# Dummy matmuls between the opening dummies and the first cumulative sum of a gated-linear-attention and expert kernel

## The chip, the cores and the metric

The kernel runs on one core of one Trainium2 chip. The metric is the device time of one execution in microseconds (us). The engines are TensorE (PE; its weight loads are listed as PEld), VectorE (DVE), ScalarE (ACT), GpSimd (POOL) and SyncE (SP), which issues the DMAs of this kernel in order.

## What is computed

Two stages follow each other: a recurrent attention with a decay for every channel, over 4 batches x 8 heads x 768 steps x 48 channels, and a feed-forward block with a squared ReLU over its 3072 x 384 output.

```python
def _attn_ref(q, k, v, alpha):
    state = np.zeros((B, H, D, D))
    for t in range(S):
        state = alpha[:, :, t, :, None] * state + np.einsum('bhd,bhe->bhde', k[:, :, t], v[:, :, t])
        y[:, :, t] = np.einsum('bhd,bhde->bhe', q[:, :, t], state)
    return y

def _moe_ref(x, w_in, w_out):      # x 3072x384, w_in 384x2048, w_out 2048x384
    r = np.maximum(x @ w_in, 0.0)
    return (r * r) @ w_out
```

## The kernel before

**Chunks.** The 4 x 768 steps are cut into 24 chunks of 128 steps. In a chunk the decay becomes a cumulative sum: ACT takes the logarithm of alpha, PE multiplies it with a triangle of ones (`e_p0`), ACT takes the exponentials A and 1/A of the sum, and DVE scales q with A (`qA_s`, L431) and k with 1/A (`kI_s`, L434). PE transposes both (L241), ACT or DVE copies the transposes out (`qkT`, L369 and L371), PE forms the scores (`sc`), DVE masks them (`sm`, L472), and PE multiplies them with v, adding the part of the running state (`st`). The result is copied (`xn`), transposed and copied again (`xT_big`).

**The first four chunks** belong together: their alpha is one load in two halves, laid out so that each chunk occupies 32 of the 128 partitions, four steps to a partition. ACT takes the logarithm of each half (L324, into a part of a `gT` tile), and each chunk's cumulative sum is four accumulating matmuls of 32 rows and 384 columns against the stationary `tri` (tile name of `tri4`). The sums of chunks 0 and 1 are the first real work of PE; they wait for both logarithms. Two PSUM banks (`GLA_BANKS`, banks 0 and 1) serve all attention work, so the sums of chunks 2 and 3 wait until a bank has been read.

**Feed-forward.** Groups of token tiles go through `x @ w_in` (banks 2 to 4), ReLU on ACT (L576), square on DVE (L584), and `@ w_out` (banks 4 to 2). The weights come as float32 through four staging buffers shared with the first alpha load, and are cast by DVE or ACT (L292, L294) into `w_in_b` and `w_out_b`; a weight piece's load is issued only when the buffer that it reuses has been cast. The first four chunks' q, k and v are loaded ahead of the weights.

**Order.** A planner (`Plan.run`) simulates all engines with durations written into the operations, and sorts the operations by planned start; `plan.order` is then issued engine by engine in exactly that sequence. Operations carry a planned `start` and `dur` in us. A DMA load of the first alpha has a planned duration of 1.18 us, a latency of 2.0 us and an earliest start of 0.6; a joint logarithm has 0.7 us, ACT's latency is 0.14 and the slack in front of PE 0.05.

**Dummies.** In front of all planned work PE gets seven matmuls of 128 x 512 zeros (`warm`) into bank 4, whose result nobody reads. In the emission loop at the end of the kernel, between two consecutive PE operations, further dummies of 256 columns are issued: as many as fit, at 0.11 us each, into the planned gap less 0.2 us. This ends with the first `@ w_out` operation. `pe_end`, the planned end of the previous PE operation, starts as None, so that nothing is issued in front of the first one. PE instructions are recorded at the helper's line, L238 for matmuls and L241 for transposes.

## Time and profile before

| what | value |
|---|---|
| median of 3 runs | 194.79 us (193.36 to 195.24) |
| the profiled execution, its own time | 194.11 us |
| its span, first to last instruction | 192.4 us |
| mean granted TensorE clock | 0.973 |
| PE's share of the chain that ended last | 79% |
| HBM read, written | 25.17 MB, 4.72 MB |

The span is the time between the first and the last instruction of the profiled execution; the 1.71 us to its own time lie outside. A busy share is the time in which an engine had at least one instruction under way; matmuls are pipelined, and the ends shown are modelled. The granted clock is TensorE's as a share of full speed, where the profiler recorded a change of it. In a timeline line the columns are start and duration in us, engine, line, operation, output and input tiles, their shape and how many; a bracket gives the idle time in front and what ended it.

### The profile page before, as it was taken

To read this page: it belongs to the slowest core of one execution; us is meant where nothing else is said; L and a number is where in the kernel's file an instruction comes from. 1 tells how busy PE (TensorE), PEld (TensorE's weight loads), DVE (VectorE), ACT (ScalarE), POOL (GpSimd) and SP (SyncE) were. 2 spreads that over 40 slices of the span, in tenths; PEclk is the share of its full clock that TensorE was granted. 3 is DMA by queue.
4 is the path that set the end of the run, shared out by engine and by line. 5 is a ranking of instruction groups with operands and counts; after the bars stand their busy time and mean duration, and the time that the engine had idled before them with its cause. 6 is when DMAs were issued, how large, how long until landed. Compare 5 with 4: busy or idle time off the path is not lost.

```text
span 192.4 us, 4966 instructions
## 1 busy us (share of the span) xinstructions
PE 182.6 (95%) x1946; PEld 132.3 (69%) x1947; DVE 127.9 (66%) x280; ACT 125.1 (65%) x289; POOL 17.7 (9%) x43
## 2 busy tenths in 40 slices
PE   6599899999998999999999999999999999999992
PEld 2256664566886788867868868867868768768651
DVE  1356988883799897967758758758757767734200
ACT  4654698917896778966956956956955845718310
POOL 8122000001102111112110110110110000000000
PEclk9855999999999999999999999999999999999999
DMA  6999689898999899999999998460110110111012
GB/s 182 222 217 283 245 250 309 202 306 173 243 202 203 175 237 187 217 215 222 212 215 237 189 218 178 95 174 3 43 44 2 42 45 0 44 41 44 22 59 82
DMA packets 104327, 30.20 MB, mean 157 GB/s; under 512 B 96240, under 2 KB 103152, under 8 KB 104304
## 3 DMA queue, kind: packets, MB, share of 16 engines
q1 hardware_dynamic: 104304, 29.89, 66.4%
q8 instruction: 15, 0.25, 0.5%
q14 instruction: 8, 0.07, 0.1%
HBM read 25.17 MB, written 4.72 MB: 155 GB/s over the span
## 4 chain that ended last, share of the span: by engine, by line
PE 79%; DMA 12%; ACT 3%; DVE 2%; issue 1%; SPq 0%; POOL 0%; POOLq 0%; ACTq 0%
PE bank L238 65%; PE bank L241 7%; DMA wo<-in_moe_w_out_dram 7%; PE sc L238 4%; DMA vt<-in_v_dram 3%; DMA at<-in_alpha_dram 2%; PE st L238 2%; DVE gT L584 1%; DVE w_out_b L292 1%; DVE sm L472 1%; ACT qkT L369 1%; ACT xn L369 1%; ACT gT L324 0%; ACT w_in_b L294 0%; POOL vb L388 0%
## 5 line engine op out<-in xcount | busy, mean ns | idle before, releaser
L238 PE MATMUL bank<-xT_big,w_in_b 128*128 128x256 bf16 (+3 forms) x587 | 75.3, 270 | 0.3
L238 PE MATMUL bank<-w_out_b,gT 128*128 128x384 bf16 x384 | 71.4, 326 | 0.0
L576 ACT ACTIVATE r<-bank 128x512 bf16<-128x512 f32 (+2 forms) x100 | 57.0, 585 | 17.6 <-PE bank L238 14.8
L238 PEld LDWEIGHTS <-w_in_b 128*128 128x128 bf16 x588 | 49.7, 97 | 10.3 <-issue 0.7
L238 PEld LDWEIGHTS <-gT 128*128 128x128 bf16 x400 | 35.7, 98 | 19.2
L584 DVE TENSOR_TENSOR gT<-r 128x512 bf16<-128x512 bf16 (+2 forms) x100 | 39.2, 419 | 14.6 <-ACT r L576 14.5
L472 DVE TENSOR_TENSOR sm<-sc,utri_b 128x512 bf16<-128x512 f32 x48 | 30.8, 683 | 4.8 <-PE sc L238 4.8
L616 ACT COPY ob<-bank 128x384 f32<-128x384 f32 x23 | 11.0, 478 | 24.0 <-PE bank L238 24.0
L431 DVE TENSOR_TENSOR qA_s<-qt,A 128x384 bf16<-128x384 f32 x24 | 13.7, 570 | 18.8 <-ACT A L408 18.8
L388 POOL CAST vb<-vt 128x384 bf16<-128x384 f32 x24 | 13.0, 543 | 124.3 <-DMA vt<-in_v_dram 77.0
L371 DVE COPY qkT<-bank 128x1024 bf16<-128x1024 bf16 (+1 forms) x23 | 15.0, 655 | 6.7 <-PE bank L241 6.5
L238 PEld LDWEIGHTS <-qkT 64*128 64x128 bf16 (+1 forms) x272 | 11.1, 97 | 7.2 <-issue 2.7
L408 ACT ACTIVATE A<-bank 128x384 bf16<-128x384 f32 x24 | 11.9, 498 | 5.0 <-PE bank L238 5.0
L434 DVE TENSOR_TENSOR kI_s<-kt,Ainv 128x384 bf16<-128x384 f32 x24 | 13.5, 563 | 0.0
L497 ACT CAST sb<-st 128x384 bf16<-128x384 f32 x20 | 9.5, 477 | 6.0 <-DVE st L492 5.7
L369 ACT CAST xn<-bank 128x384 bf16<-128x384 f32 x24 | 11.5, 481 | 2.7 <-PE bank L238 2.6
L412 ACT ACTIVATE Ainv<-bank 128x384 bf16<-128x384 f32 x24 | 12.0, 501 | 0.0
L379 ACT ACTIVATE L_s<-at 128x384 bf16<-128x384 f32 x20 | 10.4, 522 | 1.6 <-DMA at<-in_alpha_dram 1.3
L492 DVE TENSOR_TENSOR st<-st,ae_s 128x384 f32<-128x384 f32 x20 | 11.2, 558 | 0.2 <-PE st L238 0.2
L371 DVE COPY xT_big<-bank 128x384 bf16<-128x384 bf16 x22 | 7.7, 352 | 4.5 <-PE bank L241 4.5
L241 PE MATMUL bank<-ident_bf,kI_s 128*128 128x128 bf16 x96 | 9.9, 230 | 0.4 <-ACT qkT L369 0.4
L241 PE MATMUL bank<-ident_bf,qA_s 128*128 128x128 bf16 x96 | 10.0, 230 | 0.0
(52 smaller groups left out, 139.5 us busy)
## 6 DMA issues: line engine op xcount, KB each, us to landing
qt<-in_q_dram SPq DMA_DIRECT2D x24, 192.0 KB, 3.9
kt<-in_k_dram SPq DMA_DIRECT2D x24, 192.0 KB, 3.8
vt<-in_v_dram SPq DMA_DIRECT2D x24, 192.0 KB, 3.9
out_dram<-ob SPq DMA_DIRECT2D x24, 192.0 KB, 2.8
at<-in_alpha_dram SPq DMA_DIRECT2D x20, 192.0 KB, 4.1
wo<-in_moe_w_out_dram SPq DMA_DIRECT2D x4, 768.0 KB, 7.6
wi<-in_moe_w_in_dram SPq DMA_DIRECT2D x3, 768.0 KB, 8.1
at<-in_alpha_dram SPq DMA_DIRECT2D x2, 384.0 KB, 3.6
```

Source lines behind the costliest of these rows:

```text
L238: pin(nc.tensor.matmul(*a, **kw))
L241: pin(nc.tensor.transpose(*a))
L369: pin(nc.scalar.copy(out_t, in_t))
L371: pin(nc.vector.tensor_copy(out_t, in_t))
L388: pin(nc.gpsimd.tensor_copy(d["vb"], d["vt"]))
L408: pin(nc.scalar.activation(d["A"], d["pm"][:, 0:HD].rearrange("p (h d) -> p h d", h=H), AF.Exp))
L412: pin(nc.scalar.activation(d["Ai"], d["pm"][:, 0:HD].rearrange("p (h d) -> p h d", h=H), AF.Exp, scale=-1.0))
L431: pin(nc.vector.tensor_mul(qA[:, :, 0:D], d["qt"], d["A"]))
L434: pin(nc.vector.tensor_mul(kI[:, :, 0:D], d["kt"], d["Ai"]))
L472: pin(nc.vector.tensor_mul(d["sm"][:, hh], d["sc"][:, hh], utri_b.to_broadcast([P, NP, P])))
L576: pin(nc.scalar.activation(box["r"][:, 0:w], box["ph"][:, 0:w], AF.Relu))
L584: pin(nc.vector.tensor_mul(gT[g][:, f0:f0 + per, lo * P:lo * P + n], r, r))
```

## The change

`pe_end` no longer starts as None but as a planned time of 4.2 us, the constant `WARM_END`. The condition in the emission loop therefore holds for the first PE operation as well, and the loop issues dummies of 256 columns, from a fresh tile of bank 4, between the seven opening dummies and that operation. The plan is finished when this code runs, and isn't changed.

```diff
     plan.run(gate)
 
 
+    WARM_END = 4.2
     wp = banks[4].tile([P, 512], FP32, name="bank4")
     for _ in range(7):
         mm(wp, lhsT=warm[:, 0:P], rhs=warm, start=True, stop=True)
-    pe_end = None
+    pe_end = WARM_END
     for op in plan.order:
         if op.eng == "PE":
             if getattr(op, "moe", (0,))[0] == 2:
```

The loop's lines that follow, unchanged:

```python
                pe_end = None
                DUMMY = 0
            if pe_end is not None and DUMMY:
                n = max(0, int((op.start - pe_end - 0.2) / 0.11))
                if n:
                    wp = banks[4].tile([P, 512], FP32, name="bank4")
                for _ in range(n):
                    mm(wp[:, 0:256], lhsT=warm[:, 0:P], rhs=warm[:, 0:256], start=True, stop=True)
            pe_end = op.start + op.dur
        op.emit()
```

## The prediction, on record before the result

> **What bounds the kernel now.** I read the page first. TensorE (PE) is busy 95% of the span and carries 79% of the chain of waits; the slices show it saturated nearly everywhere, and its clock at half in one early stretch only.

> ```profile
> span 192.4 us, 4966 instructions
> ...
> PE 182.6 (95%) x1946; PEld 132.3 (69%) x1947; DVE 127.9 (66%) x280; ACT 125.1 (65%) x289; POOL 17.7 (9%) x43
> ...
> PEclk9855999999999999999999999999999999999999
> ```

> Each digit is 4.81 us: slices two to four hold the half clock. Next, busy time by window, finely, to find where the clock changes (columns: busy us of PE, weight loads, DVE, ACT, POOL; granted clock; DMA share; GB/s):

> ```profile
> 8.32:8.36 0.04, 0.04 (x2) 0.04 (x1) 0.04 (x1) 0.04 (x1) 0.00 (x0) 1.00 1.21 226
> 8.36:8.40 0.04, 0.04 (x2) 0.04 (x1) 0.04 (x1) 0.04 (x1) 0.00 (x0) 0.71 1.33 245
> ...
> 18.60:18.64 0.04, 0.04 (x5) 0.04 (x6) 0.00 (x0) 0.00 (x0) 0.00 (x0) 0.79 0.79 307
> ```

> The clock falls at 8.38 and is back at 18.62, 10.24 us later. I cut that stretch into thirds of 3.41 us, and lay the same cut on both sides:

> ```profile
> 1.55:4.96 3.41, 2.87 (x7) 0.85 (x6) 0.36 (x6) 1.37 (x2) 3.15 (x11) 1.00 0.92 266
> 4.96:8.38 3.42, 1.23 (x11) 0.71 (x11) 0.80 (x2) 2.16 (x5) 0.55 (x2) 1.00 1.22 225
> 8.38:11.79 3.41, 3.20 (x19) 1.77 (x18) 1.92 (x5) 1.77 (x4) 0.50 (x1) 0.50 1.21 215
> 11.79:15.20 3.41, 3.41 (x49) 2.24 (x48) 2.21 (x4) 2.29 (x6) 0.59 (x2) 0.50 1.14 214
> 15.20:18.62 3.42, 3.07 (x25) 2.24 (x25) 2.24 (x5) 1.55 (x3) 0.93 (x2) 0.50 0.99 288
> 18.62:22.03 3.41, 2.88 (x49) 2.15 (x50) 2.72 (x6) 1.83 (x4) 0.00 (x0) 1.00 1.02 384
> ```

> Last, the timeline of PE, for the paces behind those clocks:

> ```profile
> 1.26 3.17 PE L238 MATMUL bank<-warm 128*128 128x512 bf16 x7 [1.26 <-DVE warm L186]
> 6.22 0.83 PE L238 MATMUL bank<-gT,tri 32*128 32x384 bf16 x8 [1.79 <-ACT gT L324]
> 7.98 1.08 PE L238 MATMUL bank<-gT,tri 32*128 32x384 bf16 x4 [0.93 <-ACT Ainv L412]
> ...
> 10.88 1.46 PE L238 MATMUL bank<-gT,tri 32*128 32x384 bf16 x4 [0.21 <-DVE qkT L371]
> ...
> 17.13 1.49 PE L238 MATMUL bank<-warm 128*128 128x256 bf16 x6
> ...
> 19.12 1.04 PE L238 MATMUL bank<-warm 128*128 128x256 bf16 x8
> ```

> The clock column says 1.00 from the start, yet the paces correct it. Asked in finer steps, the opening dummies start at 2.51, 2.93, 3.36 and 3.79: 0.427 us for 512 columns, 1.2 columns per ns. The three sums that start at 7.98, 8.14 and 8.30 take 0.16 us for 384 columns, 2.4 per ns. So TensorE began at half pace, rose somewhere between 4.22 (end of the last opening dummy's columns) and 6.22, and fell at 8.38, after a window in which it worked 1.23 of 3.42 us (36%) although no pause in it exceeded 1.79 us. It kept full clock through the window from 18.62, with 2.88 of 3.41 (84%).

> [...]

> **The change part by part.** *How many dummies.* The plan starts its first PE operation when both halves of the joint logarithm are done: loads end at 0.6 + 2 x 1.18 + 2.0 = 4.96, the second logarithm at 5.66, with 0.14 latency and 0.05 slack 5.85. So n = int((5.85 - 4.2 - 0.2)/0.11) = int(13.2) = 13. Only this first operation is touched: every later one finds `pe_end` set as before. Plan, other engines' instructions and DMA issues stay in their order. The 13 write the bank 4 that the opening dummies wrote, on the same in-order engine; the repeated dummies of before, from 17.13 on, show no wait for that.

> *What they cost.* Cold, six take 1.49 us with about 0.21 of final drain: (1.49 - 0.21)/6 = 0.213 each. Warm, eight take 1.04 with 0.17: 0.109 each. The first starts at 4.22. All cold, the last one's columns end at 4.22 + 13 x 0.213 = 6.99; all warm, at 5.64. With the rise at 4.96, the cut's boundary before 8.38, 3.5 run cold and 9.5 warm: 4.96 + 9.5 x 0.109 = 6.00, or 6.17 with drain. The first sum started at 6.22, released by ACT, so in the profiled timing the cost is nothing: the wait of 1.79 us covers all 13. If that cover fails it is 6.99 - 6.22 = 0.77 us on the path. Other executions may rise at other times; between 0 and 0.77 I take 0.3.

> *What they buy.* The window 4.96 to 8.38 gains 1.04 us of matmul: 2.27 of 3.42, or 66%. Known: fall after 36%, hold after 84%; 66% is nearer to the hold (18 points against 30). The trace has no window between, so both ends stay in the range: no effect, or full clock from 8.38 to 18.62.

> *The worth of that stage.* Three windows hold 3.20 + 3.41 + 3.07 = 9.68 us of cold PE work, so it cannot exceed 4.84. On the chain: the third joint sum ran two of its four matmuls cold, 1.08 instead of 0.66, saves 0.42; eight transposes, 0.98 to 0.56 (four cost 0.34 with drain at 18.96 and 0.22 without), 0.42; the fourth sum, 1.46 to 0.74, 0.72; eight score matmuls, 0.54 to 0.34, 0.20. That makes 1.76 when DVE's masking of chunk 0 starts (12.99 now). From there DVE runs without pause to 17.49 on six steps, so PE's speed adds nothing along that engine. Then DVE idles 1.51 us, until the scores of chunk 2 at 18.55 (masking at 19.00). On PE's side, by the same paces, this stretch shortens by 0.55 + 0.20 + 0.15 + 0.20 + 0.25 + 0.60 = 1.95 (26 small matmuls, scores, state, two transposes, the six dummies), more than the idle time; so 1.51 is what can be had. Together 1.76 + 1.51 = 3.27 us at 19.0.

> Will the clock hold inside that stage? The work at double pace is about 4.84 us in 10.24 - 3.27 = 6.97, 69% busy, again between 36 and 84 and nearer to 84. [...]

> *How much reaches the end.* Next late are the loads. A staging buffer frees when DVE casts the first w_in piece (22.28 to 22.83), and the next piece is issued at 22.86; meanwhile the DMA engines drain. By one-microsecond windows they moved 385 GB/s at 21 to 22, 72 at 22 to 23, 29 at 23 to 24 and 152 at 24 to 25. The casts move 3.3 earlier with PE, but transfers only fill that hole of about 2.2 us. So loads come 2.2 earlier, PE wants them 3.27 earlier, and 1.1 must come out of slack. w_out: first cast done 33.05, first used 36.24; third done 41.68, used 43.52: slack 1.8, enough. Chunk loads: vt's cast ends at 38.78, its user starts 39.55: slack 0.77, loses 0.3; at 58.5 PE already waits 0.6 for a vt, with no slack. So 2.2 to 3.27 arrive; I take 2.6, about the mean less one small wait. After 60 us PE is full (40.00 of 40 us in 60:100 and in 100:140, and so on to 186), so nothing later can absorb or return it.

> Sum, against the profiled execution: 194.11 (span 192.4 and 1.71 around it) - 2.6 + 0.3 = 191.8. That execution lies 0.68 under the median of 194.79, inside the runs' 193.36 to 195.24; I don't scale, since a spread of that size would follow if before's early rise comes in only some executions, and that spread goes with the change.

> **The rivals.** *It falls anyway.* 66% is not enough, or the thinner windows behind it are not. For it: before fell with no long pause, and the 8.38 to 11.79 window is mostly transposes and 32-row sums, which at half clock were busy 3.20 of 3.41 us and did not bring the clock back, so busy time alone isn't what is counted. Against: the next cold window rose at 18.62 with only six dummies among small work. Fallen at 8.38: 194.1. Fallen at 11.79: saved 0.42 + 0.42 and about half of 0.72, some 1.2, less 0.3: 193.2. So 193.2 to 194.8 with the median's offset.

> *Late rise, slower than before.* The dummies delay the first joint sum. The last column ends at b + 0.51 x (6.99 - b) for a rise at b; this passes 6.22 when b is later than 5.42. Price 0.77 at most, at the head of the chain, where ACT, then PE wait for it; with the clock falling again nothing pays it back: 194.11 + 0.77 = 194.9, or 195.6 from the median. Against: in the profile the rise is before 6.22 even without the added work.

> *The loads take it.* The clock holds, but SP's queue, in order and with issues that last up to 4.13 us (qt at 26.36), keeps the loads where they were: the 3.27 shrink to what slack there is, 0.77 to 1.8: 192.6 to 193.6. Against: the buffers free earlier, and the 2.2 us hole is real.

> **How the numbers follow.** Hold: 0.55, 190.8 (3.27 arrives, no delay) to 192.7 (2.2, delay 0.77), likeliest 191.8. Falls anyway: 0.26. Late rise and slower: 0.12. Loads take it: 0.07. The range 190.6 to 194.8 takes in the first, second and fourth, and leaves out nearly the 0.12 and the tails. This kernel's measurement can tell about 1% from no change: 192.8 and 196.7 are the borders. Faster: the hold, less its edge, plus the better half of the loads case, 0.56. Slower by over 1% needs 1.95, more than the delay alone can give; 0.05 for the late rise together with a longer cold stretch. The rest, 0.39, lies within.

> **What would show it.** Thirteen more 128x256 matmuls between 4.2 and about 6.2, the first of them 0.213 apart, later ones 0.109; the first joint sum within 0.1 of 6.22; granted clock 1.00 through 8.38 and on to 19; the fourth joint sum about 0.7 long, not 1.46; masking of chunk 2 near 15.7, not 19.0; the DMA hole at 22 to 24 gone; PE's last matmul 2 to 3 us earlier. It is wrong if the clock falls at 8.4 or 11.8 anyway, if the first sum starts after 6.6, or if new PE waits on loads show between 30 and 60.

## The result, and the profile after

| | median, us | lowest to highest | executions |
|---|---|---|---|
| before | 194.78 | 193.13 to 196.09 | 20 |
| changed | 192.48 | 190.37 to 194.79 | 20 |

Over all 20 executions of each, the medians stand at 192.48/194.78 = 0.988: faster by about 1.2%. The ratio on record, 0.985 (95% interval 0.982 to 0.989), leaves out the six executions of the changed kernel above 193.2 us as slow ones, but by what follows these belong to it. The recorded 191.8 lay 0.7 us under the median, and the range held it.

The changed kernel's times do not scatter around one value. They fall into groups by the mean granted clock of the execution. With two repeats that are told below there are 32 executions:

| mean granted clock | executions | times, us | median |
|---|---|---|---|
| 0.999 to 1.000 | 13 | 190.37 to 192.10 | 190.89 |
| 0.989, 0.991 | 2 | 190.88, 192.37 | |
| 0.978 to 0.982 | 9 | 192.58 to 193.69 | 193.16 |
| 0.970 to 0.974 | 8 | 194.11 to 195.27 | 194.64 |

One third of before's cold stretch, 3.41 us at half clock, takes 3.41 x 0.5/192 = 0.009 off the mean, so the rows stand for none, one, two and three cold thirds.

The execution that was profiled took 193.69 us (span 192.0, clock 0.979): it is of the third group. Its page, the slices of the clock:

```profile
PEclk9957999999999999999999999999999999999998
```

Busy time by window, cut in thirds as in the prediction, but at this execution's own changes of clock (columns as there: PE, weight loads, DVE, ACT, POOL, granted clock, DMA share, GB/s):

```profile
2.84:6.25 3.41, 3.35 (x13) 1.69 (x12) 0.00 (x0) 1.68 (x2) 2.55 (x7) 1.00 1.06 279
6.25:9.66 3.41, 2.46 (x24) 1.35 (x22) 1.44 (x3) 1.84 (x5) 0.00 (x0) 1.00 1.03 203
9.66:13.07 3.41, 3.35 (x25) 1.66 (x23) 1.27 (x4) 1.81 (x5) 1.01 (x2) 0.50 1.04 203
13.07:16.49 3.42, 3.42 (x49) 2.80 (x49) 3.31 (x6) 1.98 (x6) 0.51 (x1) 0.50 1.03 208
16.49:19.90 3.41, 2.85 (x35) 2.03 (x34) 2.65 (x6) 2.29 (x5) 0.62 (x1) 1.00 0.98 293
```

Its timeline of PE, the lines that answer to those of before (the 20 `warm` are the seven opening dummies and the 13 added ones):

```profile
1.25 5.65 PE L238 MATMUL bank<-warm 128*128 128x512 bf16 x20 [1.25 <-DVE warm L186]
6.84 0.83 PE L238 MATMUL bank<-gT,tri 32*128 32x384 bf16 x8
8.62 0.81 PE L238 MATMUL bank<-gT,tri 32*128 32x384 bf16 x4 [0.94 <-ACT Ainv L412]
...
11.02 1.46 PE L238 MATMUL bank<-gT,tri 32*128 32x384 bf16 x4
```

Here the clock fell again, at 9.66, and was back at 16.49, after two thirds instead of three. The window in front of the fall had TensorE busy 2.46 of 3.41 us, 72%: more than the 66% that the prediction had hoped would do. And the first joint sum starts at 6.84, 0.62 late, without a releaser in its bracket: it stands behind the dummies. The end of PE's work came only 0.41 us earlier than in before's profile.

A second profile of the same kernel, from the repeat `e10_after` (190.52 us, span 188.8), caught an execution of the first group:

```profile
1.98:5.39 3.41, 3.35 (x11) 1.40 (x10) 0.10 (x2) 1.10 (x3) 3.16 (x10) 1.00 1.04 295
5.39:8.80 3.41, 2.46 (x22) 1.44 (x20) 1.00 (x3) 2.21 (x5) 0.12 (x1) 1.00 1.14 212
8.80:12.22 3.42, 2.87 (x33) 1.66 (x32) 2.25 (x6) 2.51 (x7) 0.50 (x1) 1.00 1.01 201
12.22:15.63 3.41, 2.90 (x54) 2.35 (x53) 3.41 (x8) 2.23 (x6) 0.81 (x2) 1.00 1.12 222
```

The clock stayed at full speed, behind a window with TensorE busy for the very same 2.46 us. So busy time alone does not tell these two apart. Its timeline, with the first sum only 0.20 late and the fourth at the full pace:

```profile
1.25 5.23 PE L238 MATMUL bank<-warm 128*128 128x512 bf16 x20 [1.25 <-DVE warm L186]
6.42 0.83 PE L238 MATMUL bank<-gT,tri 32*128 32x384 bf16 x8
8.20 0.81 PE L238 MATMUL bank<-gT,tri 32*128 32x384 bf16 x4 [0.95 <-ACT Ainv L412]
...
10.42 0.82 PE L238 MATMUL bank<-gT,tri 32*128 32x384 bf16 x4
...
15.87 0.40 PE L238 MATMUL sc<-qkT 64*128 64x128 bf16 x8
```

**What orders the windows.** Between two changes of the clock in the first 20 us lie 3.41 to 3.42, 6.82 to 6.83 or 10.24 us in the six profiles in which it fell early (before, after, `e1_again`, `e2_rows32`, `e4_half`, `e7_26`): one, two or three of the thirds that the prediction cut. So a third is taken here as the window of the count. That is the author's assumption: the traces show the lengths of the stretches, not what the clock is decided on. Weight each matmul's columns by the rows that it uses. In the window 5.39 to 8.80 of `e10_after`, about 8.7 dummies at the full pace (256/2.4 = 0.107 us each, at the 384 columns in 0.16 us of the joint sums) are 0.93 us of the whole array; the 12 joint sums take 0.16 us each on 32 of 128 rows, 0.48 us by weight; together 1.41 of 3.41, 0.41 by this rough count. In the window 6.25 to 9.66 of after, only 4.7 dummies were left (0.50), the same sums (0.48), and five transposes (0.27): 1.25, or 0.37. In before, 4.96 to 8.38: sums alone, 0.42, or 0.12. Done from each matmul's own start, which moves a share by about 0.01, over the profiles of this study:

```
weighted share of a window at full clock in these profiles, and what came after it
fell:  0.12 before   0.20 e2_rows32   0.28 e4_half   0.28 e7_26   0.38 after   0.39 e1_again
held:  0.40 e9_fill32   0.41 e3_fill   0.42 e10_after   and all others, 0.43 to 0.99
share of a window at half clock: stayed low up to 0.65, rose 0.75 to 1.01
```

Unweighted, the same matmuls fill 0.80 of after's window that fell and 0.60 of one in `e10_after` (12.22 to 15.63) that held; so the order is wrong without the rows, and right with them. Without the transposes it is wrong too: 0.18 held (`e10_after`, 8.80 to 12.22, 0.43 with them) and 0.35 fell (`e1_again`). So this count takes transposes like other matmuls.

This is an order found in the twelve profiles of this case, by the author's own count, not a mechanism or a threshold that was measured step by step. Its edge lies in the narrow gap between 0.385, which fell, and 0.403, which held, and a record of a matmul can be missing (`e10_after`'s page has 1959 of them, after's 1960). Rows were tested apart, in `e2_rows32` and `e9_fill32`.

The rise, where the record of the clock begins, came at 4.96 in before's profile, and at 6.25, 5.96 and 5.39 in the three profiles of the changed kernel, although the seven opening dummies start at 1.25 or 1.26 in all of them. In after's the paces agree: the dummies start 0.213 us apart up to 6.14 and 0.109 apart from 6.31 on. So the windows lay differently in these four executions. The rise at 6.25 left 4.7 dummies to the next window, and the clock fell; the rise at 5.39 left 8.7, and it held.

The dummies do a second thing. Of before's 57 executions beside the experiments, only 17 have a mean of 0.965 to 0.982, like the one that the prediction was worked out on. The other 40 have 0.996 and more and still took 193.34 us or longer; none of them was profiled, but an execution of this kind was (`e5_fill_only`, below), and its clock did not rise before 19.26. All 32 executions of the changed kernel are either in the groups of a fallen clock or, at 192.10 us and less, faster than any of before's. So behind the 13 dummies the early rise seems to come every time.

### The profile page after: what moved, and what is told of

Same layout as the page of the kernel before. It is cut to its first block, busy times and chain, and to the rows that moved or that the text cites. A ratio compares the mean times of both kernels' runs of the same rounds, so it can differ in the third digit from the quotient of the medians.

```text
span 192.0 us, 4993 instructions
## 1 busy us (share of the span) xinstructions
PE 184.0 (96%) x1960; PEld 133.4 (69%) x1960; DVE 127.2 (66%) x280; ACT 125.2 (65%) x289; POOL 17.6 (9%) x43
## 4 chain that ended last, share of the span: by engine, by line
PE 87%; ACT 4%; DMA 4%; DVE 3%; issue 1%
PE bank L238 73%; PE bank L241 8%; PE sc L238 4%; DMA wo<-in_moe_w_out_dram 4%; PE st L238 2%; ACT r L576 1%; DVE gT L584 1%; ACT xn L369 1%; DVE w_out_b L292 1%; DVE sm L472 1%; ACT qkT L369 1%; ACT sb L497 0%; ACT w_in_b L294 0%; DVE st L492 0%; ACT A L408 0%
## 5 line engine op out<-in xcount | busy, mean ns | idle before, releaser
L238 PE MATMUL bank<-xT_big,w_in_b 128*128 128x256 bf16 (+3 forms) x588 | 75.4, 270 | 0.2
L238 PE MATMUL bank<-w_out_b,gT 128*128 128x384 bf16 x384 | 71.4, 326 | 0.0
L238 PEld LDWEIGHTS <-w_in_b 128*128 128x128 bf16 x588 | 49.7, 97 | 10.3 <-issue 0.7
L238 PEld LDWEIGHTS <-gT 128*128 128x128 bf16 x400 | 35.7, 98 | 19.2
L584 DVE TENSOR_TENSOR gT<-r 128x512 bf16<-128x512 bf16 (+2 forms) x100 | 38.6, 412 | 14.9 <-ACT r L576 14.8
L371 DVE COPY qkT<-bank 128x1024 bf16<-128x1024 bf16 (+1 forms) x23 | 15.0, 655 | 6.8 <-PE bank L241 6.6
L238 PEld LDWEIGHTS <-qkT 64*128 64x128 bf16 (+1 forms) x272 | 11.1, 97 | 7.1 <-issue 2.4
L412 ACT ACTIVATE Ainv<-bank 128x384 bf16<-128x384 f32 x24 | 12.0, 499 | 0.0
L238 PE MATMUL bank<-warm 128*128 128x256 bf16 (+1 forms) x48 | 10.3, 357 | 1.3 <-DVE warm L186 1.3
L371 DVE COPY xT_big<-bank 128x384 bf16<-128x384 bf16 x22 | 7.7, 352 | 4.2 <-PE bank L241 4.0
L238 PE MATMUL bank<-vb,sm 128*128 128x48 bf16 x192 | 9.3, 185 | 0.9 <-DVE sm L472 0.9
## 6 DMA issues: line engine op xcount, KB each, us to landing
qt<-in_q_dram SPq DMA_DIRECT2D x24, 192.0 KB, 3.9
kt<-in_k_dram SPq DMA_DIRECT2D x24, 192.0 KB, 3.8
vt<-in_v_dram SPq DMA_DIRECT2D x24, 192.0 KB, 3.5
out_dram<-ob SPq DMA_DIRECT2D x24, 192.0 KB, 2.6
at<-in_alpha_dram SPq DMA_DIRECT2D x20, 192.0 KB, 4.1
```

Source lines behind the costliest of these rows:

```text
L238: pin(nc.tensor.matmul(*a, **kw))
L371: pin(nc.vector.tensor_copy(out_t, in_t))
L412: pin(nc.scalar.activation(d["Ai"], d["pm"][:, 0:HD].rearrange("p (h d) -> p h d", h=H), AF.Exp, scale=-1.0))
L584: pin(nc.vector.tensor_mul(gT[g][:, f0:f0 + per, lo * P:lo * P + n], r, r))
```

## The experiments

All ratios are to before, run beside. A clock mean needs care: in an execution whose clock never rose early, no change is on record before the late rise, and the time in front of it is shown as 1.00. `e5_fill_only` shows that below. Means of 0.995 to 0.999 can come from a fall behind PE's last matmul: in after's profile PE's work ends at 188.48 and the clock falls at 190.57, which alone takes 1.42 x 0.5/192 = 0.004 off its mean. So "held" means a clock of 0.995 or more and, since sums at half clock cost time (eight took 1.47 us instead of 0.83 in `e5_fill_only`), a time under 192.7 us.

**e1_again** and **e10_after**: the changed kernel, unedited.

> The changed kernel once more, for the granted clock of each execution and a second trace. My theory: what the change does depends on where the clock's windows of about 3.41 us fall against the start, which differs from execution to execution; so the times again form groups by the length of the half-clock stretch: no cold window near 190.8 us (clock 1.00), one near 192.4 (0.991), two near 193.2 (0.98), three near 194.5 (0.973), with about half of the executions in the first group and a median of 192 to 193. The rival, that the change shortens every execution by about the same and the spread is noise, expects times that do not follow the clock.

Measured: 193.37 us median of six, 0.994 of before's 194.47. Two held (191.21, 191.75), one at 0.980 took 192.64, three at 0.970 to 0.974 took 194.11 to 195.27. The groups are there again, the rival is out; the median lies above what was expected, since the draw had more falls.

**e2_rows32**: the added dummies on 32 rows.

```diff
+    opened = False
...
+                r = P if opened else 32
                 for _ in range(n):
-                    mm(wp[:, 0:256], lhsT=warm[:, 0:P], rhs=warm[:, 0:256], start=True, stop=True)
+                    mm(wp[:, 0:256], lhsT=warm[0:r, 0:P], rhs=warm[0:r, 0:256], start=True, stop=True)
+                opened = True
```

> The 13 added dummies work on 32 of the 128 rows: same number, same columns, same time on TensorE. If the clock follows how much of the array works (my theory, since in the changed kernel it fell after a window with TensorE busy 72%), the added dummies count a quarter: nearly no execution stays at full clock, the median is 194 to 195.5, like before or a little later. If it is enough that TensorE is occupied (rival, the way my prediction counted), it is like the changed kernel: median 192 to 193, half of the executions near 190.8.

Measured: 195.37 us median of 12, ratio 1.004 (1.000 to 1.007); none held. The window behind the early rise, by window:

```profile
4.29:7.70 3.41, 2.54 (x22) 1.75 (x22) 0.08 (x1) 2.02 (x4) 1.24 (x3) 1.00 1.19 233
7.70:11.12 3.42, 3.04 (x17) 1.73 (x16) 2.08 (x5) 1.93 (x6) 0.50 (x1) 0.50 1.26 222
```

TensorE is busier (2.54) than in the window that held in `e10_after` (2.46), and the clock fell. Five executions with a mean of 0.972 to 0.973, like the 17 of before's 57 with an early rise behind the opening dummies alone, took 193.41 to 194.86; the other seven (0.996 and above) took 195.32 to 196.52. None of the seven was profiled; if their clock never rose early, as their means and times say, the 13 dummies ran at half pace, and the price of the delay is seen: median 195.9 against 194.5 for before's executions of that kind (40 of 57), 1.4 us.

**e3_fill**: the 13, and seven more in front of the third joint sum.

```diff
+            if getattr(op, "gla", None) == 2:
+                wp = banks[4].tile([P, 512], FP32, name="bank4")
+                for _ in range(7):
+                    mm(wp[:, 0:256], lhsT=warm[:, 0:P], rhs=warm[:, 0:256], start=True, stop=True)
             pe_end = op.start + op.dur
         op.emit()
```

> The changed kernel plus 7 dummies of 256 columns in the wait before the third joint sum (0.94 us idle in the profile of after). My theory: the window that holds the joint sums is the weak one, and 0.76 us more of whole-array work lets the clock hold in most executions: more than three quarters at clock 0.995 or above, median 190.5 to 191.5. Rival (the wait for the exponentials is on the path and the work of the opening decides): the share stays at about half, median 192 to 193.5, with up to 0.7 us more where the dummies run cold.

Measured: 192.31 us median of six, ratio 0.990 (0.984 to 0.995). Three held (190.95 to 191.56); the others are at 0.981 to 0.991 (193.06 to 193.61), and none at 0.973. Half, not three quarters: the expectation missed. The window that was filled is strong now (0.59 by weight in its profile), but the next one stands at 0.41, hardly over the edge. The weak place had moved on.

**e4_half**: six added dummies (`n = 6` at the first operation).

> 6 added dummies in place of 13. My theory: fewer phases find enough work in the window, so the share of executions at full clock throughout lies between before's (none expected) and that of the changed kernel (about half): 10 to 35%, median 193.3 to 194.4. Rival (any work that ends the 1.8 us pause will do, since a pause is what makes the clock fall): about as with 13, median 192 to 193.

Measured: 193.85 us median of 12, ratio 0.997 (0.994 to 1.000), 192.66 to 195.23. None held (three at 0.997 took 193.79 to 194.38, like before's executions without an early rise), where 10 to 35% were expected. In its profile the window behind the rise has a weight of 0.28. Six dummies bought 0.3%, and in no execution of 12 the held clock that 13 dummies gave in 13 of 32.

**e5_fill_only**: before, with the seven in front of the third sum and none in the opening gap.

> The kernel before plus the 7 dummies in front of the third joint sum, without the 13 in the opening gap. My theory by now: a stretch of 3.41 us lets a full clock fall when its matmuls, weighted by the rows they use, fill less than about 0.40 of it, and raises a half clock when they fill more than about 0.75. Then early rises stay as rare as in before (a third), and the window behind them has 0.12 + 0.22 = 0.34, still too little: no execution near 191, median 194 to 195.5, ratio to before 0.998 to 1.006. Rival (the wait before the third sum is the weak place, whatever stands before): a third of the executions hold, near 191.

Measured: 194.89 us median of 12, ratio 1.001 (0.997 to 1.004), as expected, none near 191. Its profile also shows the trap in the clock's mean. The page, and the timeline of PE:

```profile
PEclk9999999999999999999999999999999999999999
```

```profile
6.19 1.47 PE L238 MATMUL bank<-gT,tri 32*128 32x384 bf16 x8 [1.77 <-ACT gT L324]
7.60 1.67 PE L238 MATMUL bank<-warm 128*128 128x256 bf16 x7
9.20 1.46 PE L238 MATMUL bank<-gT,tri 32*128 32x384 bf16 x4
```

The slices say full clock from the start, but eight sums take 1.47 us instead of 0.83, and four 1.46 instead of 0.81. This execution ran at half pace until 19.26, where its record begins.

**e6_fill_more**: the 13, and fills in four places.

```diff
+        p0.fill = {2: 7, 3: 2}.get(s, 0)
+        p1q.fill = {1: 3}.get(s, 0)
+        p1k.fill = {2: 4}.get(s, 0)
...
+            if getattr(op, "fill", 0):
+                wp = banks[4].tile([P, 512], FP32, name="bank4")
+                for _ in range(op.fill):
+                    mm(wp[:, 0:256], lhsT=warm[:, 0:P], rhs=warm[:, 0:256], start=True, stop=True)
```

> The changed kernel plus 7 dummies before the third joint sum, 2 before the fourth, 3 before the transposes of q of chunk 1, 4 before those of k of chunk 2. My theory: the later windows gain 0.05 to 0.2 each, so that no phase falls under 0.40: at least 80% of the executions at full clock once risen, median 190.6 to 191.6. Rival (these waits are shorter than the dummies, which then delay the chain): clock held, but times of 191.5 to 193.

Measured: 191.52 us median of six (191.09 to 192.54), ratio 0.985 (0.981 to 0.989). All six held, at 0.997 and above; as expected.

**e7_26**: 26 dummies in the opening gap.

> 26 dummies in the opening gap in place of 13. The clock should hold nearly always behind them; the first joint sum starts 1.35 to 2.0 us after 6.22 instead of 0 to 0.8. If a delay at the head of the chain reaches the end undiminished (my theory): all executions near 190.6 + 1.4 to 2.0, 192.0 to 192.9, with little spread. Rival (later stages have slack for it, the first loads being what bounds): 190.6 to 191.5.

Measured: 194.35 us median of 12 (193.65 to 195.39), ratio 0.999 (0.997 to 1.002). The expectation failed: 11 of 12 are at 0.979 to 0.982, two cold thirds. By window, and the timeline:

```profile
4.56:7.97 3.41, 3.41 (x34) 2.71 (x33) 0.00 (x0) 1.17 (x2) 0.97 (x3) 1.00 1.21 220
7.97:11.38 3.41, 2.16 (x21) 1.15 (x17) 2.26 (x6) 2.51 (x6) 0.79 (x1) 1.00 1.19 212
```

```profile
7.43 0.83 PE L238 MATMUL bank<-gT,tri 32*128 32x384 bf16 x8
```

The window with the dummies held; the one behind it, by weight 0.28, did not. The first sum is 1.21 later than before's 6.22. In this profile the two together cancel the gain: a delay at the head, paid for a clock that falls one window later.

**e8_one_tile** and **e11_best**: as e6_fill_more, with the 13 in the opening dummies' own tile (no new tile at the first operation).

> As the kernel with fills in four places, and the first 13 dummies continue in the opening dummies' tile of bank 4. In the profile of after the first added dummy waits for the drain of the opening ones and starts at 4.48, not 4.22. My theory: that 0.26 us goes, so the first joint sum comes 0.1 to 0.26 earlier in executions that rise late; median 0.1 to 0.3 under the kernel with a fresh tile. Rival: no difference that shows (within 0.2).

Measured: 191.34 us median of six (190.56 to 192.24), ratio 0.983 (0.979 to 0.987); all six held. In its trace the first added dummy starts at 4.21, in after's at 4.48: with no new tile, the wait of 0.26 is gone. On the time, 0.18 between the medians lies within the spread; whether it shows there stays open.

**e9_fill32**: as e8_one_tile, the 16 fills on 32 rows.

> The kernel with fills in four places and one tile, with the 16 fill dummies on 32 rows in place of 128: same number, columns and time, a quarter of the rows. My theory (rows count, threshold near 0.40): the clock falls again in some phases, share at full clock throughout 40 to 75%, median 191.7 to 193.3, at least 0.5 us above the whole-array fills beside it. Rival (it is enough that TensorE is occupied and its pauses are gone): as with whole-array fills, 190.9 to 191.7, all at full clock.

Measured: 193.28 us median of six (191.15 to 195.49), 0.994 of before's 194.40. Three held, one took 193.92 at 0.980, two 194.47 and 195.49 at 0.971 and 0.974. Beside it:

> The changed kernel on the same chip, for comparison. 35 to 60% of the executions at full clock once risen, those at 190.3 to 191.9, the others 192.3 to 195; median 192.2 to 193.5.

> Fills in four places and one tile, once more, beside the changed kernel on one chip. My theory: at least 80% at full clock, median 190.9 to 191.8, 0.8 to 2 us under the changed kernel's. Rival (the first result came from favourable phases): median within 0.5 us of the changed kernel's.

Measured on the same chip: the changed kernel 192.19 us median of six (190.52 to 195.00), two held and one at 0.989; fills of the whole array 191.77 us (190.74 to 193.29), ratio 0.986 (0.981 to 0.991), all six at 0.999 and above; five held, and the sixth, 193.29 at 0.999, can't be told from an execution without an early rise. The medians differ by 0.42, less than the 0.8 expected, and six executions don't separate them. What is separated is the clock: whole-array fills kept it in 17 of 18 executions (e6_fill_more, e8_one_tile, e11_best), the changed kernel in 13 of 32. Fills of the same length on 32 rows kept it in three of six, which points the same way, with few executions.

Over both its runs, the version with fills and one tile has a median of 191.5 us (190.56 to 193.29), against 192.6 (190.37 to 195.27) for the changed kernel over its 32. Its gain is in the worst executions, not in the best: in the profile of `e11_best` the first joint sum starts at 6.92, 0.70 late, and PE's last matmul comes 2.66 earlier than in before, against 3.59 in `e10_after`. That delay is not the dummies': PE had waited 0.42 us for ACT's logarithm.

## Why the prediction came out as it did

**Direction, range and count were right.** 13 dummies, at 0.213 cold and 0.109 warm, with nothing else reordered. That 191.8 came near the median is in part luck: it was meant for a held clock, and 12 of the 13 held executions lie under it, while the median is that of a mixture with fallen ones. Of the prediction's own signs of being wrong, after's profile shows two outright: the clock fell again (at 9.66), and the first sum started behind 6.6 (at 6.84). The third, PE's waits on loads between 30 and 60, shows as a longer wait behind DVE (0.58 and 0.33 us for 0.21, below). Its guess on the spread, that before's early rise comes in only some executions, fits 17 of 57.

**The step that failed is the one that judged whether the clock holds.** The prediction took TensorE's busy share, 66%, and called it nearer to the 84% that held than to the 36% that fell. After fell at 72%, `e2_rows32` at 74%, and `e10_after` held at 72%. The rival *it falls anyway* had the right doubt: "busy time alone isn't what is counted", from the cold windows that were busy 3.20 of 3.41 us without a rise. What orders the profiles is busy time weighted by rows: 0.38 and 0.39 where the changed kernel fell, 0.42 where it held, just at the edge. So the two cases that the prediction weighed at 0.55 and 0.26 are not alternatives: both occur, 13 and 19 in 32 executions (in the three profiles, held behind the rise at 5.39, fallen behind those at 5.96 and 6.25), and the median of 192.48 lies between them.

**The price of a held execution was nearly right.** 191.5 without a delay, 191.8 with 0.3; measured 190.37 to 192.10, median 190.89. Of its terms: the stage up to the scores of chunk 2 was to give 3.27; in `e10_after` they start at 15.87 instead of 18.55, 2.68 earlier, with the first sum 0.20 late, so 2.88. The carry to the end was to shrink to 2.6; it grew, to 3.59 at PE's last matmul. The term that was too small is the loads': they were to come 2.2 earlier, but here the third `w_out` piece was issued at 31.29 instead of 34.62, 3.33 earlier, and its cast had no wait. The hole in the DMA traffic did close (399 GB/s at 21 to 22, 375, 362 and 262 in the three microseconds behind), as the prediction had it, and the waits of before disappeared with it: 2.69 earlier at the first `w_out` matmul, 3.07 at the 33rd, 3.82 at the 65th. By window, before's stretch of 8 us around the wait at 58, and the same work in `e10_after`:

```profile
52.00:60.00 8.00, 7.42 (x125) 6.36 (x124) 7.88 (x19) 6.69 (x16) 0.66 (x1) 1.00 0.89 201
```

```profile
49.00:57.00 8.00, 8.00 (x139) 6.77 (x136) 7.88 (x20) 7.21 (x17) 0.51 (x1) 1.00 0.96 214
```

TensorE's 0.58 us of idle time is gone.

**In the profiled execution of after, the loads did take it.** It was 0.61 ahead at the first `w_out` matmul and 0.26 behind at the 33rd. The prediction gave the third `w_out` piece 1.8 us of slack, counted to its user on TensorE. The slack that ends first is on DVE, where the mask stands behind the cast. Before's profile already showed that none was left there; this cast waited for its load there too, and PE for the mask:

```profile
40.72 0.96 DVE L292 CAST w_out_b<-wo 128x1536 bf16<-128x1536 f32 x1 [0.28 <-DMA wo<-in_moe_w_out_dram]
43.40 0.27 PE L238 MATMUL bank<-vb,sm 128*128 128x48 bf16 x4 [0.21 <-DVE sm L472]
```

DVE's timeline in after:

```profile
40.98 0.96 DVE L292 CAST w_out_b<-wo 128x1536 bf16<-128x1536 f32 x1 [1.15 <-DMA wo<-in_moe_w_out_dram]
41.86 0.56 DVE L492 TENSOR_TENSOR st<-st,ae_s 128x384 f32<-128x384 f32 x1
42.33 1.28 DVE L472 TENSOR_TENSOR sm<-sc,utri_b 128x512 bf16<-128x512 f32 x2
```

and TensorE's waits behind it:

```profile
43.06 0.27 PE L238 MATMUL bank<-vb,sm 128*128 128x48 bf16 x4 [0.58 <-DVE sm L472]
43.66 0.27 PE L238 MATMUL bank<-vb,sm 128*128 128x48 bf16 x4 [0.33 <-DVE sm L472]
```

In `e10_after` that cast started at 37.66 with no wait. `e1_again`'s profile shows what this wait costs apart from the clock: its clock has the same course as after's (one warm window, two cold), and both start the scores of chunk 2 at 17.95 and the first `w_out` matmul at 35.63. But SP's issue of a kt load in front of the `w_out` piece took 3.33 us instead of 4.25, the piece was issued at 33.13 instead of 34.11, and the cast did not wait:

```profile
39.75 0.95 DVE L292 CAST w_out_b<-wo 128x1536 bf16<-128x1536 f32 x1
```

Its 33rd `w_out` matmul came 1.25 us before after's, its last matmul 1.05, and the times differ by the same 1.05 (192.64 and 193.69). Why the issue took longer in after stays open.

**Late rise** was right in that it occurs: the rise came at 6.25 in after's profile, behind the 5.42 from which the prediction saw a delay. Its price is the first joint sum at 6.84 instead of 6.22 in after's profile, and 1.4 us in the executions of `e2_rows32` that by their means never rose early. That before's repeated dummies "show no wait" did not carry over to this place: the first added one starts at 4.48, not 4.22, and at 4.21 where `e8_one_tile` leaves out the new tile.

## What to carry to other kernels

Where the clock's mean splits the executions of one kernel into groups, a change's gain is the share of executions that it moves between groups (here 13 of 32, with a median of 190.89 us against before's 194.78); look at the clock of each execution before taking a median as one effect. To hold the clock, these runs suggest counting matmuls by columns and rows used, in each window of the clock's record (3.41 us here) and at every possible place of it (the rise lay at 4.96 to 6.25). With 13 dummies on 32 rows the clock held in none of 12 executions (`e2_rows32`), with the whole array in 13 of 32; and when one weak window had been filled to 0.59 (`e3_fill`), the next stood at 0.41 and only three of six held. Dummies belong where TensorE waits anyway, and no more of them than the wait holds at half pace (0.213 us each here, in a wait of 1.79): the 13 put the first joint sum at 6.84 in after's profile, 0.62 late, and 26 put it at 7.43 in `e7_26`'s, 1.21 late.
